# Gated mix of dilated attention and a spectral filter: a new issue order for the second half of the kernel

## The chip, the cores and the metric

The kernel runs on one core of a Trainium2 chip. The metric is device time in microseconds (us). The kernel before took 452.81 us as a median of 3 runs (452.49 to 456.78).

## The reference

The input x has S = 2048 rows of D = 640. Branch a is attention with 32 heads of 20: each row attends to 8 rows at distances 0, 2, ..., 14 behind it. Branch b is a 2-D Fourier transform, a multiplication by a complex weight, and the transform back. A gate mixes them.

```python
qkv = (x @ wqkv).reshape(B, S, 3, H, Dh)             # H = 32, Dh = 20
idx = pos[:, None] - (jnp.arange(8) * 2)[None, :]    # mask = idx >= 0
logits = einsum("bhsd,bhswd->bhsw", q, k[idx]) * Dh ** -0.5
o = einsum("bhsw,bhswd->bhsd", softmax(where(mask, logits, -1e9)), v[idx])
a = o.reshape(B, S, D) @ wo
b = irfft2(rfft2(x) * (w_r + 1j * w_i), s=(S, D))
g = sigmoid((x * gate_w).sum(-1, keepdims=True))
return g * a + (1 - g) * b
```

## The kernel before

All 16 row blocks j lie as row = 16 p + j on the 128 partitions p, so that a block is every 16th row. The work has these stages, most of which overlap.

1. **qkv.** TensorE (PE) multiplies x by wqkv, in a first half for even j and a second for odd j, each in four groups of heads. ScalarE (ACT) copies each bank to a tile `ev` and stores it to a DRAM tensor `qkvd`. Until about 239 us PE does little else.
2. **attention** (`attend`), for eight heads groups per half, named by unit and letter (7a, 7b, 6a, 6b, 5a, 5b, 4a, 4b are those of the second half, in the order in which they run). For each, `kt`, `vt` (600 KB each) and `q` are loaded from `qkvd` into a ring of six buffers; the products `pr` and their sums `L` are made mostly on VectorE (DVE); a softmax follows; the products `pv` are made on GpSimd (POOL) and summed to `o` on DVE, which is stored to a DRAM tensor `od`.
3. **frequency stage** (`freq(g)`, 16 steps, in the order 1, 2, 3, 0, 4, ..., 15; from 238 to 350 us). A step makes, in PE, `v` and `u` (bank 0 and bank 1), in ACT a copy `vs` of v, in DVE `ab` = u + vs and u − vs, which frees u's bank, in PE `x` and `z` from ab and a table `mm`; ACT copies x to the first third of a tile `P`, and multiplies x and z by a sign into `X`, whose two halves two DMAs on ACT's queue (160 KB each, 64 partitions) exchange into the rest of P. Then POOL multiplies P by the weight `wp` of this step (642 KB, loaded by SyncE, SP, into one of two buffers) and adds two thirds of it, DVE multiplies z by wp, subtracts P's last third (z−P in the text), and forms two sums `s`; a small ACT step completes s; PE makes `g` from s, and ACT copies g to `zg`. Step 0 makes `ix` and `iz` in place of the exchange.
4. **project_even**, mixed into it: `ot` is loaded, transposed on PE (`oTp`), split into two parts `oT` by ACT and DVE, multiplied by wo (`woa`, `wob`), scaled by the gate on ACT, and stored to `ad`.
5. **spatial** (350 to 407 us) makes the rows of b from zg (`oa`, `ob`, `ha`, `hb`); the even blocks are finished there with what `ad` holds.
6. **project_odd** (407 to 447 us) does the output projection of the odd blocks and the last stores.

The order of all this isn't the order in which the code calls the engines. Each call of an engine is recorded as one of 3614 operations (`Plan.record`); `Plan.order` then takes them from that list by a table of positions, `ORDER`, a compressed text of bytes; and `Plan.issue` runs them in this order, with the framework's own scheduling switched off. The framework puts in the semaphore waits that the data and the buffers ask for. Each engine has one queue that it works off in order, and a DMA waits in the queue of the engine that issues it: `kt`, `wp`, `mm`, `ot` and the stores of `o` on SP's, `vt`, `q`, P's exchange and the stores of `ev` on ACT's (`ON_ACT`). Which buffer or bank a tile gets is settled when it is recorded, so ORDER doesn't change that: x is always bank 2, z banks 3 and 4 in turn, g bank 5, the projection bank 6.

In the profile all recorded calls show one line, L400, except those of `Engine.run`, which are L177. So the profile is read by the names of tiles.

Of the kernel before, what the change touches and what calls it, by code (L numbers as in the profile page):

```python
# [17 lines left out]
S, D = 2048, 640  # L18
# [213 lines left out]
%*_v{Ta_^3=d<&1(R>`cY~)FfJAaBz1ZK0I<N^-e7(pzkO~FPz<-dP(x(IlwVBqSbRRT5rYgu1T6G{2<I~O<a=YYl0Jk$QP{l|_cUTx1sL~IU#-qKQc=BZ{n4m`EvZF&VD8v<QobTp<#G}S-$H`Uf3  # L232
lV6!!5tQ?X+VqEQ;48Q$_J_73PWOHP+BCYo8Y-^CjsRGKe*zWp49~VEfz?XhfDFHGoCqv^_Kpn;y4>(MBVz{ny;&9IO*)|MYVG9JncXGFPoic<`y=IEWte%CmWSp+Y(?B){u46!4sOair&o<;_Iq~K
3>`-kmHW$~uf>&2Jr05V5nspNt;nTvSO|#fz%QF~8X35h0g$l!JgO6RW!C68drMU&X5A6P=$Nr$+3jJPJ}uOj?=*n19-86hl;LN8Hhf<GxhI&winTZQ>2x;|-suR*5NzR*Uwo9z+eSs6vga>nZOwBG
vLfUmcstXVX;$<mV<B7Oc8{(9Pt{1C13guny)&_~q%$t2kz5)^-d8^>eAsZ7EM8Oz;y?j{zH-yTJHejC*-FFaYuSxIKkree?rYC2bW3W_yQgR@e#A)4&MXBfmOcKy<E&!!vdXd)`5M^&Pegrjt213<
Q1^7bAKaX_6D=5&6d7EIuzq~__@DxEGE=WG9(#$x0LH^-vD``kI}fUGW#|^h!u*`Ow@P$|J8B%p1zm`(grJuCIIT_GfcsAk1)l!3HXU)~?U7qYNO_Gt=w3t$jG%dd9Ksr=<wp6LB)ZQ%4A4SWObh;*
RA!!7t1p4B+tN0OgLygfxAScXYQ}vlM0eBD7jso~Egme7wu9n*bYoWZaMo7mVp<GIX3?0zZYCA!ock-4_(6CTPAT38Wm{e?u^lZ`vF^p9erqZ-v89)N$1@>Xn{+x$m;6b?f;>#{pWCaqKGa+g1*;||
y<<yQ!&N=^1CqrpZk90@j&LGJlMyy|(BBp8S4Z|duoIc_X4s{yRYN!c6BFn)jKjNf+n>dr`qn_B!u=Q;@co)GBq81xMJ~cha0hAP0y)*5W4}Cj@=It+Cf${fI(`t`M89Nxs$Vl%p}!usDSWi-uamq9
L1H6jJsz(u8~3MqodIHL;4J<ohmAh|OK6kI=+dnk16>ll98S}@JD_@ZhOMd^K9&;5ptMQZBLWPdk`^UuL+0omK_Fii#f4`Xo+AK;_(LC7aA~!Fl<nAx#H(0DQzYEM>)N5b`vSea*aqcSl%7Uj`|-fA
FUi#-xiXER^66kMImz$qNq=rK!`8u~G0J@ZJ@P-@fTNQsIW?MNXZwXEsg6Q(=D|UndsuDw=~=(?v4L<eD8lBDP<p7no7pdR>YOVFQMJn{rAGTH^V&3iq8BYdi_<gCcvH5KRaOs15p^lK%&*eDlACo=  # L240
C}*H&-g&0j)St4GreIZ#TG<*aimDSC%*Wm!vxsIxMEGFWrL0@IrF;1NGOduo<C2jV{m$zFYTsK?^-^@_gB`nBms`c+Qah%wZdv=fl@uAEJw%WhqN^<m*#OCC_}dQq_(TG(ABO)+HgKRq$=Gh)F1+Y`
lHF?dsJb7>dEXJ&4d~Gs#`=ro&!=@;z<{yT^bd}5Be+?zs#~Ztr(l5sjrQR7p?SdQQWAX~@^a@zEiy=Jv6Qpe?xiC<;1YQ8Dmtm%aps*@&NhcJr6S;SMZB$?V4JHAtJ|wpQN97*0>>cg@94#?97E>z
pU?&YRWjdFygm~3=6}?Kf~mXd(yFa%=t&aIYHN?fCEkN+dp1y%Le$TZH5w~(eNLzW@Ff=olKJzr&i$JZF3vp|$YJx@d<+Am+-cw+ve-2t*@=hYn6MRi@LbzaaNrVM1`Z;P41*KiKeL?G@uR^-1MZ5x
&-8t7Du9l>se=sPCxLnNh;^qjLG5`BXp?n1mOQv_foF~PmrIp0URDZ9y{AxbCEqx~gc22Kl55n9iKb3pmM2AFl?9s<%V_(F=6&<AHu-VupN1gQiTtv^$=dzAPsK$unsZLvi(M{|@Mz<GZ0vG`-R8y^
bv7z~Pg0O1gkLeUqgQeq5%2C9*y`mtKUd+!)|0D2@BdqV%JHrxltS?Np2LNOjj#QLWP*&p4jikEFT4al``Go?Z{aiaW^}2=gL^VNQjc}d4svyvlHJEWdz*EN&g_ArzPjuAQS1(S$C_w%7ZL_JLexHo
6Nw65Rol(|>9&}$FY9Hfijtts{9>(rn|i6b10=LY`g-?C(t1(9$sqZ0Pd+5CM$WOG0Jg>}Y_c&Glxk0Odj1Gzb;g+@my_})V2Rc%Nz|V44};O+VX~t%-R<B?XKlQm38e~G=F)4bm$ln-fu}=g!uu-G
IKE@Ycb{9`szhQr(gLm`%k>!i3IdZbL>|0ftSvP1#mIxlvXh}b9V*=7i#LRT_9KBgCyF3iP9s+^s8;{19)Lqti(_Z}%cQw&3E<#UCl%!M_^OH1bF#vSJJH1%@-m~}l-EXb`>QMDbJR1<??VJ#_D+S|
??F>fX_^NI<G5n+MgCe4u+1FXcTLFiPK-*-@1Sq@L=T{l182WS+Oxj#uuSg{fI(h!=ZeSZwm<`)>5FR?WShdG9839FRJIn1L_=AM@N(se=&hn2tB88b;iE<#$}VZFq((Q)8~YVvIs~+jLJd3k1I^ig
e!Vj#k`-!U!L?8Ec{a#98LT5<5pd1T<I-RrilniF3~47HcQ1`iO1<O;g1m*{1_;S#Jy-{rb|4l(8c7UFl^~}jU}pt--wC&3>=)and8<&7T#&>10000000I6Oyf^>={WXEXr~nH50ssI2003E9
"""  # L250


# [725 lines left out]
```

## Time and profile before

| | us |
|---|---|
| median of 3 runs | 452.81 (452.49 to 456.78) |
| profiled execution | 453.08 |
| its span (first to last instruction) | 451.0 |
| PE busy | 435.0 (96%), 2576 instructions |
| DVE busy | 409.1 (91%), 519 |
| POOL busy | 363.2 (81%), 318 |
| ACT busy | 214.9 (48%), 593 |
| mean granted clock of PE | 1.000 |

The time is 2.08 us longer than the span; the profile doesn't show that part. Busy time is an average over stages with different limits, and matmuls are pipelined with modelled ends, so the idle time in front of single PE instructions, and what ended it, says more than the 96%. A wait for several semaphores is put down to the one that came last by the profile, which can be the wrong one where the named engine had long been done.

### The profile page before, as it was taken

The numbers are of one execution on the slowest core, as the hardware profiler recorded it, in microseconds if no ns is written. First come the engines' busy times: TensorE is split into PE (matmuls) and PEld (weight loads), VectorE is DVE, ScalarE is ACT, GpSimd is POOL, SyncE is SP. The second block draws the span as 40 slices with busy tenths as digits, with TensorE's granted clock in tenths as the row PEclk, the third lists the DMA queues.
The fourth block names the chain that finished last, engine by engine and source line by source line (L and its number), as shares of the span: only waits on it lengthen the run. The fifth ranks groups of instructions, "written<-read, shape, count | busy, mean of one in ns | idle before, by whom it ended". The sixth has DMA issues, their size and how long they took to land. (4 is left out here: it accounts for less than half of the span.)

```text
span 451.0 us, 7548 instructions
## 1 busy us (share of the span) xinstructions
PE 435.0 (96%) x2576; PEld 384.9 (85%) x2576; DVE 409.1 (91%) x519; ACT 214.9 (48%) x593; POOL 363.2 (81%) x318
## 2 busy tenths in 40 slices
PE   9999999999999999999998989799998999999996
PEld 6888878888888888899886869698977899989996
DVE  4999999999999999999999776898988999887775
ACT  5543144462325355245547657486754665552110
POOL 1247987999999897989998695689988998889920
PEclk9999999999999999999999999999999999999999
DMA  8999797989487999978969969899864732276653
GB/s 324 389 340 331 236 383 221 326 242 367 128 220 233 297 286 302 308 202 260 294 194 293 329 204 278 235 305 263 254 198 130 248 108 69 81 227 197 187 200 118
DMA packets 73958, 110.60 MB, mean 245 GB/s; under 512 B 21297, under 2 KB 50993, under 8 KB 73921
## 3 DMA queue, kind: packets, MB, share of 16 engines
q1 hardware_dynamic: 40192, 69.16, 47.7%
q10 hardware_dynamic: 32816, 36.97, 27.4%
q0 software_dynamic: 912, 4.00, 2.4%
q8 instruction: 20, 0.33, 0.3%
q14 instruction: 18, 0.14, 0.1%
HBM read 72.34 MB, written 32.84 MB: 233 GB/s over the span
## 5 line engine op out<-in xcount | busy, mean ns | idle before, releaser
L400 PE MATMUL qkv<-w,xo 128*128 128x480 f32 (+1 forms) x480 | 116.5, 388 | 0.3 <-ACT zg L400 0.2
L400 PE MATMUL qkv<-w,xe 128*128 128x480 f32 (+1 forms) x474 | 106.6, 382 | 1.1 <-ACT ev L400 1.1
L400 PEld LDWEIGHTS qkv<-w,xe 128*128 128x128 f32 x474 | 89.2, 189 | 16.8 <-ACT ev L400 2.0
L400 PEld LDWEIGHTS qkv<-w,xo 128*128 128x128 f32 x480 | 88.5, 189 | 13.6 <-ACT zg L400 0.7
L400 ACT COPY ev<-qkv 128x480 f32<-128x480 f32 x64 | 34.8, 560 | 56.4 <-PE qkv L400 47.2
L400 PE MATMUL wob<-wo,oT 128*128 128x320 f32 x240 | 50.8, 327 | 0.0
L400 PE MATMUL woa<-wo,oT 128*128 128x320 f32 x240 | 50.4, 327 | 0.0
L400 POOL TENSOR_TENSOR P<-P,wp 128x963 f32<-128x963 f32 (+1 forms) x16 | 35.2, 2199 | 16.9 <-DMA P<-X 11.3
L400 PEld LDWEIGHTS woa<-wo,oT 128*128 128x128 f32 x240 | 37.7, 189 | 0.9 <-DVE oT L400 0.5
L400 PEld LDWEIGHTS wob<-wo,oT 128*128 128x128 f32 x240 | 37.8, 188 | 0.6 <-issue 0.2
L400 POOL TENSOR_TENSOR fx<-fx 128x158 f32<-128x158 f32 (+1 forms) x16 | 12.3, 784 | 25.4 <-DVE fx L400 18.5
L177 PE MATMUL ob<-gt,zg 64*128 64x161 f32 (+2 forms) x160 | 27.7, 327 | 0.0
L177 PE MATMUL oa<-gt,zg 64*128 64x161 f32 (+1 forms) x160 | 27.6, 327 | 0.0
L400 ACT CAST oT<-oTp 128x384 fp32r<-128x384 f32 (+1 forms) x32 | 13.1, 426 | 28.7 <-PE oTp L400 17.0
L177 PEld LDWEIGHTS oa<-gt,zg 64*128 64x128 f32 x160 | 23.7, 186 | 3.1 <-issue 0.7
L400 PE MATMUL g<-mm,s 128*128 128x128 f32 x150 | 24.8, 278 | 1.3 <-ACT s L400 0.7
L400 POOL TENSOR_TENSOR w<-raw,w 128x480 fp32r<-128x480 f32 (+1 forms) x20 | 25.9, 1306 | 0.0
L400 PEld LDWEIGHTS g<-mm,s 128*128 128x128 f32 x150 | 21.8, 190 | 3.6 <-ACT zg L400 1.0
L400 DVE TENSOR_TENSOR oT<-oTp,oT 128x384 fp32r<-128x384 f32 (+1 forms) x32 | 15.4, 488 | 9.6 <-ACT oT L400 9.3
L400 PE MATMUL u<-bt,zc 128*128 128x240 f32 (+2 forms) x96 | 21.0, 324 | 3.0 <-DVE ab L400 3.0
L177 PEld LDWEIGHTS ob<-gt,zg 64*128 64x128 f32 x160 | 23.8, 186 | 0.0
L400 ACT CAST w<-raw 128x480 fp32r<-128x480 f32 (+1 forms) x30 | 17.4, 594 | 12.6 <-DMA raw<-in_wqkv 6.4
(307 smaller groups left out, 1131.2 us busy)
## 6 DMA issues: line engine op xcount, KB each, us to landing
qkvd<-ev ACTq DMA_DIRECT2D x32, 480.0 KB, 4.9
wp<-in_ws SPq DMA_DIRECT2D x16, 642.0 KB, 5.6
raw<-in_wqkv SPq DMA_DIRECT2D x25, 240.0 KB, 5.4
fx<-in_x SPq DMA_DIRECT2D x8, 641.0 KB, 7.1
ot<-od SPq DMA_DIRECT2D x16, 320.0 KB, 4.1
P<-X ACTq DMA_DIRECT2D x30, 160.5 KB, 4.2
fd<-fx POOLq DMA_DIRECT2D x6, 640.0 KB, 5.3
f<-fd SPq DMA_DIRECT2D x6, 640.0 KB, 6.4
```

Of the source, the lines that this page charges most:

```text
L177: getattr(self.real, name)(*a, **k)
L400: p.dve.memset(w, 0.0)
```

## The change

Only the text of `ORDER` differs. The first 1765 of the 3614 operations stay; of the 1849 behind them 1729 stand at another position, half of them by 5 places or less, nine in ten by 32 or less, the farthest by 343. Every engine has the same instructions as before. Each engine's first difference lies between 223.9 us (PE) and 230.2 us (DVE) in the time of the kernel before.

```diff
 ORDER = """
-{Wp48S^xk5{}S0j0stWa8~^|S5YJf5;2b*)YFz*T0sAKZbW)=m>G~>ja#c?We=xxA
...
+{Wp48S^xk5{}S0j0stWa8~^|S5YJf5;2b*)UtItI0sAKZbW)=m>G~>ja#c?We=xxA
...
```

Three places show what moved. The number in a name is that of the step, or the unit and letter of the heads (`pr5a4`: heads 5a, rows 4); the last number counts tiles and stays the same.

The first is on DVE, in steps 5 and 8 of the frequency stage. Before:

```order
L400 TENSOR_REDUCE o7b4_497<-pv7b6_499 128x160
L400 TENSOR_TENSOR z5_676<-z5_676,wp5_665 128x321
L400 TENSOR_TENSOR z5_676<-z5_676,P5_674 128x321
L400 TENSOR_TENSOR pr5a4_538<-kt5a_532,qbank_63 128x1280
L400 TENSOR_TENSOR ab8_710<-u8_709,vs8_708 128x321 x2
L400 TENSOR_TENSOR s5_686<-P5_674,z5_676 128x5x64 x2
```

After, on the same engine:

```order
L400 TENSOR_REDUCE o7b4_497<-pv7b6_499 128x160
L400 TENSOR_TENSOR ab8_710<-u8_709,vs8_708 128x321
L400 TENSOR_TENSOR z5_676<-z5_676,wp5_665 128x321
L400 TENSOR_TENSOR pr5a4_538<-kt5a_532,qbank_63 128x1280
L400 TENSOR_TENSOR ab8_710<-u8_709,vs8_708 128x321
L400 TENSOR_TENSOR z5_676<-z5_676,P5_674 128x321
L400 TENSOR_TENSOR s5_686<-P5_674,z5_676 128x5x64 x2
```

Both halves of ab of step 8, and pr5a4, now stand ahead of the instruction that reads P of step 5. On POOL, two multiplies pv6a0 have moved to the place ahead of P of step 5 (and what they need, L6a times s6a, ahead of P of step 3). On SP the load of kt5b has moved from behind the load of wp6 to behind that of wp2, 11 places earlier.

The second place is ACT's queue between qkv and the frequency stage, where vt6a is loaded. Before:

```order
L400 ACTIVATE X2_621<-z2_620,sign_325 128x321
L400 COPY zc0_637<-zg_211 128x48x4
L400 COPY vs3_625<-v3_624 128x321
L400 ACTIVATE zc0_637<-zg_211 128x48x4
L400 DMA P2_618<-X2_621 64x642 x2
L400 COPY P2_618<-x2_619 128x321
L400 DMA vt6a_501<-qkvd_64 128x1200
L400 DMA qkvd_64<-ev4_6_323 128x6x160
```

After:

```order
L400 COPY ev4_4_320<-qkv4_5_321 128x6x80
L400 DMA qkvd_64<-ev4_4_320 128x6x160
L400 DMA q5a_534<-qkvd_64 128x640
L400 COPY qbank_63<-q6b_518 128x160
L400 DMA vt6a_501<-qkvd_64 128x1200
L400 COPY zc1_602<-zg_211 128x384
```

The load of vt6a has moved from behind P of step 2 to the copies of the last qkv banks, ahead of P of step 1. The load of vt6b, which stood between P of step 1 and P of step 2, now stands behind P of step 3, ahead of vs5.

The third place is ACT's queue near the end of the frequency stage. Before:

```order
L400 ACTIVATE s12_780<-z12_769,P12_767 128x1
L400 COPY vs15_801<-v15_800 128x321
L400 ACTIVATE ya8_848<-woa8_849,g_73 128x320
L400 ACTIVATE X14_797<-z14_796,sign_325 128x321
L400 DMA P14_794<-X14_797 64x642 x2
L400 COPY P14_794<-x14_795 128x321
```

After:

```order
L400 ACTIVATE s12_780<-z12_769,P12_767 128x1
L400 DMA vt5b_549<-qkvd_64 128x1200
L400 ACTIVATE ya8_848<-woa8_849,g_73 128x320
L400 ACTIVATE X14_797<-z14_796,sign_325 128x321
L400 COPY P14_794<-x14_795 128x321
L400 COPY vs15_801<-v15_800 128x321
L400 DMA P14_794<-X14_797 64x642
L400 COPY qbank_63<-q4a_566 128x160
L400 DMA P14_794<-X14_797 64x642
```

The load of vt5b stood behind the last g of the stage; now it stands ahead of P of step 14, whose two DMAs have two ACT copies more ahead of them, and one between them. Elsewhere in PE's order, x of step 4 stands ahead of z of step 4, and a v matmul of step 3 ahead of x of step 2; on DVE, t of step 0 stands behind z−P of step 3.

More of the change, by code (lines that the diff above doesn't have):

```diff
@@ L222 @@
 ORDER = """
-{Wp48S^xk5{}S0j0stWa8~^|S5YJf5;2b*)YFz*T0sAKZbW)=m>G~>ja#c?We=xxAfB@%${{m#x=b59`IdyTU{vq(yT@9sNe+BS{#HY+m)y=f!_RR8qRRBGA*}EW<uG2O+6A~}&R!D}&rV+x2jv1iJ
+{Wp48S^xk5{}S0j0stWa8~^|S5YJf5;2b*)UtItI0sAKZbW)=m>G~>ja#c?We=xxAfB@%${{m#x=b59`IdyTU{vq(yT@9sNe+BS{#HY+m)y=f!_RR8qRRBGA*}EW<uG2O+6A~}&R!D}&rV+x2jv1iJ
 <-;gAir31;1Wf;>N>_o7_jkA<(T8Z}8f9+iVn*m~XGw&Dh4Q!g^!a-g;gRa_JDi6k#N9Iq<cZ2&JtcN76xX8*H9m++$L@A2#7kr>_z#tF%`KR?`)4zIcgHuNs+E`A0h0RujinI`1a|acnWK|Ere?@m
@@ L234 @@
 3>`-kmHW$~uf>&2Jr05V5nspNt;nTvSO|#fz%QF~8X35h0g$l!JgO6RW!C68drMU&X5A6P=$Nr$+3jJPJ}uOj?=*n19-86hl;LN8Hhf<GxhI&winTZQ>2x;|-suR*5NzR*Uwo9z+eSs6vga>nZOwBG
-vLfUmcstXVX;$<mV<B7Oc8{(9Pt{1C13guny)&_~q%$t2kz5)^-d8^>eAsZ7EM8Oz;y?j{zH-yTJHejC*-FFaYuSxIKkree?rYC2bW3W_yQgR@e#A)4&MXBfmOcKy<E&!!vdXd)`5M^&Pegrjt213<
-Q1^7bAKaX_6D=5&6d7EIuzq~__@DxEGE=WG9(#$x0LH^-vD``kI}fUGW#|^h!u*`Ow@P$|J8B%p1zm`(grJuCIIT_GfcsAk1)l!3HXU)~?U7qYNO_Gt=w3t$jG%dd9Ksr=<wp6LB)ZQ%4A4SWObh;*
-RA!!7t1p4B+tN0OgLygfxAScXYQ}vlM0eBD7jso~Egme7wu9n*bYoWZaMo7mVp<GIX3?0zZYCA!ock-4_(6CTPAT38Wm{e?u^lZ`vF^p9erqZ-v89)N$1@>Xn{+x$m;6b?f;>#{pWCaqKGa+g1*;||
@@ L238 @@
[L238 to L249, printed above, removed]
+vLfUmcstXVX+;I|zA<K_j}gV#Y!WNY{{+th<9!`zZp9Qbuyo3|?%M^X%JMtja)#YJ?0Wu?C3|7heNpzzNVsdyf^jS^d5EL;7!gZ{mpMNB4Eog0mKm1?%&?YhifjiJ+WsK*uke%>;o$nSuZ~QtdR8qZ
@@ new lines @@
+sFn@jY!=scvP^xj45X(oupXhV$gAes*6pTQn(V?ZWTVQSv(G5kFQap|AAIxumA2W@CJkzeNN5n|+8(ysoh631UroY@8($&y9R=O|iVF=#r{j#dC@1n#yU%L3g-{aE^{PYf@<?MUvV3J1ch>NDVK|M&
+dn(8qarH>hSZAgOeZR7rwZKP{_47puSwoU2geH)WmFDLyM*)ux%>W?fNuw9Y>_*Yp@s=}+%((t1G)Bt<m<p=;x*oLUVGTOZUGY|2P&CY*e2p2IEU>Nk93;q46;oyV`=mD{`!jzZ2((~d-Ay}Xn(4qP
+{u|v7Ep-V&<lh#+O*E110f1EX5P;DW4}7za_e9YE-UBV-iKQcp{fAo|)Qt>FdPeJ*t1NYaY(%EjPpqezPYJy~iNowP$Spp|;Mkj<MR;)rj0yG)e1?lWKiJ26)_0%_gLukJ3Z+Ei3;RQ)Ow?kdvG-`{
+kvSMk%|*!N!wKJJuO_!BS~L8>=T-gF;bt51C(lFb876-+s?V39+YMk&TA=`2iW76p;mnd+|0Is2;ClLRpuVY<;Gg;~Nt%bMT$^3M@FHkD*ctz%HOA(<6!CeW6w24_(c`G96ev!D7YTX>#}qBhN+(gO
@@ new lines @@
+D6I)E-Q(zEOFg(EGC_%!KI-tz3tyEU=PUFjbdr5N@MSdVlXp>RE`N6aLU@gPS!zhH2X92XagxqA)En;ljspP<*Xp>((O3TMy|p>erYZFk{@{!xn@<F@8r~{Usxd@3za<dn%fmMsFK#mI0HNI^7&oj?
+Bb+5*(po9`WEB(P(5v}|W#=Z5HW7&Pd0hmr`+dk*!ksPK4SfZ*-11}V(6{&7x=ZSSVA|2SQzQHhmq!oHBzs<EiFlO)wsQ>9xhH>Pry?pXU^SLLmcb17wX?DrW#RPtg1<Ri#7N}1+3CAX!t&!<WPuX-
+L~=fl?`q@pefc@o@5%_bSQQ*iB>@!rYq|yKRwJO1hi`pgm=vjYSC?v{lF|PodnoL^)sW59LjO0_6gAtf(mLwlRb6S~&+utyN?;?BiTafqd<p=N3E~r2wCLTkaU}-+gq(pwKc10`tJ#Fa-i_J2GWIXz
+q9G7!4|`s26XmGRiPB;S={E<f(GZsdM%2b|h@Ah9(2r}nWrB1D0G_w5#$-#p>Hm~|t>IByRG;1i>8gb>TYOa|6j)vzmThH4F>9&=Y)qs{v(R(-G@i0aKFSxw?O_eIg;Uu?HK0o}EuR7w$oAC=lAF|l
@@ new lines @@
+Uq2G{S}o`&C9Cy>I4=2Z_}%*z0j%7k;Vs}ezH`g%I!)7ml<OVF_+Pc3eFt<vbstX%(HpljI9pJ<;8y=KYXU7Jed9(`F@X%5!9X=}d{M$%);50y6*3M4mGQ+i*OCSk@Lho51J}SPvWK#wo0eyIg4Mh5
+ArMG`{LCPTz&dX4(zOnev>+fF)l9Wy`91XZNpG=g(9+fz3`P>)DxvOsBA(uHr%9ZIC8%5P=Wwftm3TX|(7Qr6jLid)eM=*1)ERJ4$+Pp~LQN!QEkABxNfN&WYLR&ibUGd<j79GfhRU6Im4JDHyr~9q
+R%t#2X<kA;fAc>^XKpP+!N0(VjKeV4Dn!ftztv}fmURWB?tCBpdJmTv^QUb5b+fP*>v$C&!>A{5T{8hV`vLAtiA>e~)0Ohg%~G$-1ci68aQ^+Gb!;yj${a^3`->_^94w>UFYWxj^9Y);lsMc(OZ)j`
+EtKRbu9!RqtPb7P*CY)M&q*;}j6cq(+(?gfe#P2K>^f*orVGgYF2iEIex++}>Th4+!khxWfqF&pq+X1V4ShUzUNUwRhW)9aCS*dslj+0WZR1D`E*ZxVO(gZhZ_%VMMx1>$v$lllaeN35t@bybU;Vh;
@@ L250 @@
+BmMg>ElH2Oi2x#A*KI)A@J<68kK@T_>^|NcqT=m~pPkdk%eE#5y0ZR%A_jdRD|&kTraT~NbIv5b84cJ>uC+jZz#`<uq4}Z1-`Qsu<Y{1<;B@h-e>rHSh6<@`NGOXJAWD4f*5bT^P#HU4l)21RJiDG&
+dW9zDN~Nq_l}cm+TAY$l`+Sc^?t_@)olOLQOy3HA0&G9E1B;JspnIO}Ie8_cl?P^;q>T`08!Wx8-Gg`h{D0V5W~T71WgRn22><{900HwDyf^>=BPJhxr~nH50ssI2003E9
 """
```

## The prediction

> **What bounds the kernel now.** I read the busy times first, then the stretches, then the waits of the busiest engine, and last what stands behind each wait.
>
> ```profile
> PE 435.0 (96%) x2576; PEld 384.9 (85%) x2576; DVE 409.1 (91%) x519; ACT 214.9 (48%) x593; POOL 363.2 (81%) x318
> ```
>
> TensorE (PE) does matmuls in 435.0 of 451.0 us. The order of its instructions is the same up to 223.9 us, so all that the change can do is done behind that. (Where a time is given for an instruction at its new place, it is the time at which its new neighbours ran before.) These are eight stretches from 225 us to the end; the columns are start:end, length, busy time of PE, of its weight loads, of VectorE (DVE), ScalarE (ACT) and GpSimd (POOL), the granted clock, the busy share of the DMA engines and GB/s.
>
> ```profile
> 225.00:245.00 20.00, 19.27 (x95) 16.19 (x93) 20.00 (x20) 11.93 (x40) 18.78 (x17) 1.00 0.77 252
> 245.00:262.00 17.00, 14.95 (x81) 12.37 (x80) 12.15 (x22) 9.54 (x28) 12.68 (x9) 1.00 0.94 276
> 262.00:287.00 25.00, 21.33 (x135) 18.92 (x136) 20.29 (x35) 16.51 (x52) 17.25 (x17) 1.00 0.84 251
> 287.00:328.00 41.00, 41.00 (x269) 37.23 (x267) 37.14 (x61) 29.05 (x84) 35.36 (x27) 1.00 0.89 268
> 328.00:351.00 23.00, 20.18 (x129) 17.44 (x130) 20.35 (x32) 11.27 (x31) 20.32 (x15) 1.00 0.54 151
> 351.00:405.00 54.00, 53.85 (x505) 49.86 (x501) 50.26 (x71) 31.47 (x94) 49.56 (x40) 1.00 0.50 151
> 405.00:447.00 42.00, 41.48 (x292) 40.81 (x291) 32.76 (x70) 7.57 (x19) 24.86 (x27) 1.00 0.57 180
> 447.00:451.00 4.00, 0.39 (x3) 0.13 (x1) 0.55 (x1) 0.00 (x0) 0.00 (x0) 0.96 0.31 112
> ```
>
> Length less busy time gives PE's idle time: 0.73, 2.05, 3.67, 0.00, 2.82, 0.15, 0.52 and 3.61 us, together 13.55. The last 3.61 are the store after the last matmul, which stays. So about 9.9 us can be gained at the very most, and nearly all of it lies in three stretches of the frequency stage, 245 to 287 and 328 to 351. The clock is full there, so it takes no part. Those idle times, by instruction (start, duration, what ran, in brackets the idle time before it and who ended it):
>
> ```profile
> 241.71 0.78 PE L400 MATMUL x<-ab,mm 128*128 128x321 f32 x2 [0.73 <-DVE ab L400]
> 246.00 0.81 PE L400 MATMUL x<-ab,mm 128*128 128x321 f32 x2 [0.93 <-ACT P L400]
> 259.70 0.78 PE L400 MATMUL z<-ab,mm 128*128 128x321 f32 x2 [0.49 <-DMA mm<-in_t_mm]
> 262.97 1.35 PE L400 MATMUL iz<-ab,tbfirst 128*128 128x321 f32 x4 [1.50 <-ACT s L400]
> 285.07 0.64 PE L400 MATMUL u<-bt,zc 128*128 128x240 f32 x2 [2.62 <-DVE ab L400]
> 331.90 0.67 PE L400 MATMUL u<-bt,zc 128*128 128x240 f32 x2 [0.37 <-DVE ab L400]
> 333.07 0.81 PE L400 MATMUL z<-ab,mm 128*128 128x321 f32 x2 [0.51 <-ACT s L400]
> 345.07 0.93 PE L400 MATMUL g<-mm,s 128*128 128x128 f32 x6 [0.74 <-ACT s L400]
> ```
>
> The largest is u of step 9 at 285.07. It needs the bank that u of step 8 held, and that one is free when DVE has made ab of step 8. What DVE did then:
>
> ```profile
> 278.79 0.49 DVE L400 TENSOR_TENSOR z<-z,wp 128x321 f32<-128x321 f32 x1
> 282.23 0.50 DVE L400 TENSOR_TENSOR z<-z,P 128x321 f32<-128x321 f32 x1 [2.95 <-POOL P L400]
> 282.64 1.48 DVE L400 TENSOR_TENSOR pr5a<-kt5a,qbank 128x1280 f32<-128x1280 f32 x1
> 284.03 0.89 DVE L400 TENSOR_TENSOR ab<-u,vs 128x321 f32<-128x321 f32 x2
> ```
>
> DVE stood 2.95 us at z−P of step 5, and ab of step 8 was queued behind it though its inputs were there. What it waited for:
>
> ```profile
> 279.96 2.23 POOL L400 TENSOR_TENSOR P<-P,wp 128x963 f32<-128x963 f32 x1 [5.27 <-ACT zg L400]
> ```
>
> The releaser named, an ACT copy, had nothing to do with P; POOL stood 5.27 us for P of step 5, whose two exchanged halves were still in flight:
>
> ```profile
> wp<-in_ws SPq DMA_DIRECT2D x1, 642.0 KB, 5.0
> kt5b<-qkvd SPq DMA_DIRECT2D x1, 600.0 KB, 7.7
> P<-X ACTq DMA_DIRECT2D x2, 160.5 KB, 6.6
> ```
>
> These are the transfers issued between 271 and 273 us: 6.6 us for 160 KB beside 1.2 MB of other loads.
>
> **The change, part by part.** No instruction comes or goes, so the sum is made of waits alone.
>
> *A, u of step 9.* DVE now makes ab of step 8 before it waits for P of step 5, with pr5a between its two halves. From 278.79 the queue is 0.45 (half of ab's 0.89), 0.49, 1.48, 0.45, which ends at 281.7. PE came to u of step 9 at 285.07 − 2.62 = 282.45, so ab comes some 0.7 us before PE asks for it; I take −2.5, which leaves 0.1 at the bank. The cover is that nothing ahead of ab waits; if DVE is itself late by 3 us there, the gain is nothing, and more than the 2.62 can't be had. z−P of step 5 then runs at 281.7 or when P is ready, no later than its 282.23 of now, because kt5b no longer loads beside P, and POOL fills its 5.27 us with two multiplies pv6a that were behind.
>
> *B, iz and z around 260.* PE waits 1.50 for s of step 3 and 0.49 for a table. P of step 3 was late too, and POOL stood for it:
>
> ```profile
> 258.59 2.22 POOL L400 TENSOR_TENSOR P<-P,wp 128x963 f32<-128x963 f32 x1 [4.03 <-DMA P<-X]
> mm<-in_t_mm SPq DMA_DIRECT2D x1, 480.0 KB, 7.0
> P<-X ACTq DMA_DIRECT2D x2, 160.5 KB, 5.4
> vt6a<-qkvd ACTq DMA_DIRECT2D x1, 600.0 KB, 4.3
> ```
>
> (The two rows in the middle are issues of 251 to 254.5 us, the last one of 245 to 247.) In 245 to 262 the DMA engines are 0.94 busy at 276 GB/s: the stretch is full, and what is taken out of it moves up what is behind. vt6a now goes out near 228 us (with the copies of the last qkv banks), which takes 600 KB (614 kB) away: 614 kB / 276 GB/s = 2.2 us. The small stores that went with it stay near their places, and vt6b comes in at about 256, behind P of step 3. I take −1.5: all of iz's wait would fit in the 2.2 us, the table's 0.49 I leave, since z of step 4 now also stands behind x of step 4 and z−P of step 3. Bounds: 0, if P of step 3 is then held by POOL, which has one more multiply (L6a) ahead of it, and −2.0.
>
> *C, the two x at 241.71 and 246.00.* A v matmul moves into the first gap, worth 0.4; the second is held by ACT's copy of P, which is not moved up. Taken as 0.
>
> *D, the earlier loads.* kt5b and vt6a now share 229 to 241 with the weights of the first steps and P of step 1. ACT also issues that P's halves behind three casts and copies more. If one of the two loads falls ahead of P of step 1, it is late by the 2.2 us of 600 KB; PE needs it only through s of step 1, and DVE, which makes that, is 20.00 of 20.00 us busy there, so that its own queue decides. The engines' share of 0.77 leaves 0.23 × 20 = 4.6 us of room for the 4.4 us of both. Bounds 0 and +2.2; I take 0, by that room.
>
> *E, vt5b.* Its 600 KB were issued at 350 us, when the frequency stage was over:
>
> ```profile
> vt5b<-qkvd ACTq DMA_DIRECT2D x1, 600.0 KB, 4.3
> P<-X ACTq DMA_DIRECT2D x2, 160.5 KB, 5.5
> ```
>
> Now it goes out on ACT's queue at about 333 us, right ahead of P of step 14, whose two halves took the 5.5 us of the second row. This P is on the chain that ended last, without slack, and leads through POOL, DVE and ACT to g of step 14, for which PE waits 0.74 already:
>
> ```profile
> 334.98 5.51 DMA P<-X
> ...
> 340.65 2.27 POOL P L400
> ```
>
> What is late here is late at the end. Two prices add up. First, the halves are now issued behind the copy of x into P and behind vs of step 15, two ACT copies, later by
>
> ```profile
> 332.92 0.42 ACT L400 COPY vs<-v 128x321 f32<-128x321 f32 x1
> ```
>
> 0.84 us in all. Second, the traffic: rows with a 600 KB load near them take 7.7 (kt5b above) where this one took 5.5, at most 2.2 more. Near P of step 6, though, which was behind vt5a in the same queue, it was
>
> ```profile
> vt5a<-qkvd ACTq DMA_DIRECT2D x1, 600.0 KB, 7.4
> P<-X ACTq DMA_DIRECT2D x2, 160.5 KB, 6.7
> ```
>
> only 1.2 more, at a share of 0.84, and the share here is 0.54. I take half of the 2.2, so E is 0.84 + 1.1 = +1.9, with bounds of 0 (the ACT copies hidden by an earlier z of step 14, the traffic free) and +3.0. [...]
>
> *F, the rest.* The waits 0.37 and 0.51 near 332 hang on P of step 12, the same chain one round earlier; its multiply by wp is only moved within DVE's waiting time. Behind 351 us, PE is idle 0.67 us in 96, and the new order changes little there. 0.
>
> Sum: −2.5 − 1.5 + 1.9 = −2.1. The profiled execution took 453.08 us; less 2.1 it is 451.0. It stands 0.27 above the median of 452.81, so the forecast is 450.7.
>
> **The rivals.**
>
> *More is kept* (to about 448): vt5b hides in the idle DMA share, E is 0, C gives its 0.4 and B its 2.0. 452.81 − 2.5 − 2.0 − 0.4 = 447.9. For it speaks the 0.54 share in 328 to 351, against it that E's chain has no slack.
>
> *Nothing is left* (452.8): PE runs ahead by 2.5 us at u of step 9 and gives it back at the next thing that is not moved up with it, the chain of P of step 12, which goes through DMA, POOL, DVE and ACT in turn; POOL is 35.36 of 41.00 us busy in 287 to 328 and DVE 37.14. Against it: PE has no idle time at all there, so it is the slowest of them.
>
> *Slower* (457.2): the loads ahead of P are the mechanism, at two places. vt5b delays P of step 14 by the full 3.0, and kt5b with vt6a delay P of step 1 by 2.2, which reaches PE; P of step 3 is no earlier then (B is 0), and A keeps a third, 0.8, because DVE runs late too. 452.8 + 3.0 + 2.2 − 0.8 = 457.2. It decides from 2.5 + 1.5 = 4.0 us of delay at the two places together, where A and B are used up. For it: P's 5.4 to 6.7 us where the DMA engines are 0.84 to 0.94 busy. Against it is this row, from 241.9 to 245.9 us, where vt6b and vt6a went out on P's own queue, one ahead and one behind it:
>
> ```profile
> vt6b<-qkvd ACTq DMA_DIRECT2D x1, 600.0 KB, 4.0
> ...
> P<-X ACTq DMA_DIRECT2D x2, 160.5 KB, 2.6
> ```
>
> **How the numbers follow.** Forecast 0.44 (449.3 to 452.2); more kept 0.24; nothing left 0.20; slower 0.12. A measurement of this kernel can tell about 1%, 4.5 us: faster is below 448.3, slower above 457.3. The case "more kept" is at 447.9 and lies on the edge; with half of it and a little of the forecast's lower end, and since all the waits together would be worth 9.9, faster is 0.25. Slower by over 1% needs all that the slow rival has and a little more, 0.08. The rest, 0.67, is within. The range holds the forecast, "nothing left" and most of both others: 447.0 to 455.5.
>
> **What would show it.** In the changed kernel's profile: the wait of u for ab falls from 2.62 to under 0.3 (A); iz waits under 0.3 and P of step 3 lands some 2 us earlier (B); the transfer of P of step 14 takes 6.5 to 7.7 us and g of step 14 waits 2 to 3 us instead of 0.74 (E); the stretch 287 to 328 stays without idle time. If that last stretch shows new waits for POOL or DVE, the gain of A went there and "nothing left" holds. Wrong would be a forecast whose idle sum falls by 4 us or more, or one in which P of step 1 makes PE wait before 250 us.

## The result

The changed kernel takes 450.52 us as a median of 22 runs (448.2 to 456.03), the kernel before in the same sessions 455.06 us (451.85 to 458.75). The ratio of the two is 0.9905, with a 95% interval of 0.9884 to 0.9927: 0.95% less time, some 4.3 us, twice the 2.1 us that the prediction summed. (Slow runs, over 1.5% above the fastest of the same kernel, such as the one at 456.03, are left out of the ratios and of all counts and averages further below.) The predicted 450.7 us is nearly the measured median, but partly by chance: the 452.81 us that it started from, a median of 3 runs, lies 2.2 us under the median that the kernel before shows over more runs.

The profiled execution of the changed kernel took 453.87 us, with a span of 452.1 us and a mean granted clock of 0.996. That is 3.4 us above its own median, while the profiled execution of before (453.08 us) was 2 us below its own. So these two profiles, laid side by side, show no gain at all, and what the change does must be read wait by wait. The busy times of the changed kernel, from its page, and the stretches of it that answer to those shown of before (the last three columns are the granted clock, the share of the DMA engines and GB/s):

```profile
PE 436.8 (97%) x2576; PEld 386.0 (85%) x2576; DVE 408.1 (90%) x519; ACT 215.3 (48%) x593; POOL 363.8 (80%) x318
```

```profile
225.00:245.00 20.00, 19.93 (x98) 16.87 (x97) 19.97 (x21) 11.35 (x35) 18.10 (x17) 1.00 0.90 302
245.00:262.00 17.00, 14.90 (x82) 12.00 (x80) 12.20 (x21) 10.80 (x35) 13.31 (x9) 1.00 0.91 250
262.00:287.00 25.00, 23.27 (x134) 20.22 (x135) 20.72 (x35) 15.86 (x47) 21.10 (x20) 0.93 0.76 226
287.00:328.00 41.00, 39.74 (x256) 36.13 (x255) 35.19 (x58) 27.68 (x80) 31.09 (x24) 1.00 0.87 262
328.00:351.00 23.00, 21.20 (x139) 18.43 (x137) 21.52 (x33) 12.26 (x35) 21.12 (x17) 1.00 0.75 221
```

PE's idle time in them is 0.07, 2.10, 1.73, 1.26 and 1.80 us, 6.96 in all, where it was 9.27. In the third stretch the clock is 0.93, where it was 1.00. The main waits of PE in the changed kernel, in order of time (three more, of 0.46 to 0.58 us, stand at 304.22, 340.16 and 341.50):

```profile
246.51 0.78 PE L400 MATMUL x<-ab,mm 128*128 128x321 f32 x2 [1.10 <-DVE ab L400]
249.48 0.94 PE L400 MATMUL v<-bt,zc 128*128 128x240 f32 x4 [0.56 <-ACT vs L400]
263.26 0.81 PE L400 MATMUL z<-ab,mm 128*128 128x321 f32 x2 [1.34 <-DVE t L400]
264.43 2.22 PE L400 MATMUL iz<-ab,tbfirst 128*128 128x321 f32 x4 [0.36 <-ACT s L400]
285.04 0.57 PE L400 MATMUL u<-bt,zc 128*128 128x240 f32 x2
320.59 0.81 PE L400 MATMUL z<-ab,mm 128*128 128x321 f32 x2 [0.80 <-ACT s L400]
345.68 0.94 PE L400 MATMUL g<-mm,s 128*128 128x128 f32 x6 [0.59 <-ACT s L400]
```

The u of step 9 (at 285.04) has no wait left; it had 2.62. The iz waits 0.36 instead of 1.50, but z of step 4 just ahead of it now waits 1.34, where its table cost 0.49. It waits for DVE's t of step 0, which in the new order stands behind z−P of step 3, and that one waited 3.59 us for POOL's P in this execution. And g of step 14 waits 0.59, not more than the 0.74 of before. DVE around ab of step 8, in the changed kernel:

```profile
281.93 0.48 DVE L400 TENSOR_TENSOR ab<-u,vs 128x321 f32<-128x321 f32 x1
282.33 0.49 DVE L400 TENSOR_TENSOR z<-z,wp 128x321 f32<-128x321 f32 x1
282.73 1.48 DVE L400 TENSOR_TENSOR pr5a<-kt5a,qbank 128x1280 f32<-128x1280 f32 x1
284.12 0.48 DVE L400 TENSOR_TENSOR ab<-u,vs 128x321 f32<-128x321 f32 x1
284.52 0.49 DVE L400 TENSOR_TENSOR z<-z,P 128x321 f32<-128x321 f32 x1
```

These are the five instructions in their new order, without a stop, and z−P of step 5 no longer waits for POOL (it waited 2.95). POOL's multiply of P of step 5 has no wait either, where it had 5.27; the two pv6a stand ahead of it:

```profile
278.89 2.70 POOL L400 TENSOR_TENSOR pv6a<-vt6a,L6a 128x640 f32<-128x640 f32 x2
281.45 2.27 POOL L400 TENSOR_TENSOR P<-P,wp 128x963 f32<-128x963 f32 x1
```

### The profile page after: what moved, and what is told of

The parts are those of the page before. It is cut to its first block, busy times and chain, and to the rows that moved or that the text cites. A ratio compares the mean times of both kernels' runs of the same rounds, so it can differ in the third digit from the quotient of the medians.

```text
span 452.1 us, 7560 instructions
## 1 busy us (share of the span) xinstructions
PE 436.8 (97%) x2576; PEld 386.0 (85%) x2576; DVE 408.1 (90%) x519; ACT 215.3 (48%) x593; POOL 363.8 (80%) x318
## 5 line engine op out<-in xcount | busy, mean ns | idle before, releaser
L400 PE MATMUL wob<-wo,oT 128*128 128x320 f32 x240 | 49.7, 325 | 0.0
L400 PE MATMUL v<-bt,zc 128*128 128x240 f32 (+2 forms) x96 | 21.5, 326 | 1.0 <-ACT vs L400 0.6
```

The costliest lines, as they stand in the source:

```text
L400: p.dve.memset(w, 0.0)
```

## The experiments

Three questions: which part of the order gains, whether the early load of vt5b costs what I said, and where the other 2 us come from. All kernels below compute the same thing; only the order differs, but for one that also moves a load to another queue. A cut means: the one order up to a position in the list of operations, and behind it what is left, in the other order.

### Three parts of the order

The first three kernels put one part of the new order into the order before: up to 267 us, from there to some 290 us, and from there to 351 us.

```diff
 e1_early:   order = new[:2100] + what is left, as before
 e2_middle:  order = before[:2100] + new[:2330] + what is left, as before   (kt5b kept behind wp6)
 e3_late:    order = before[:2330] + new[:2815] + what is left, as before
```

> The new order up to the last matmul of step 0's iz (some 267 us), then the order before. It has the early loads of kt5b and vt6a and vt6b's later one, and not the new place of ab of step 8, nor the early vt5b. My sum: iz's wait of 1.50 goes, the u of step 9 still waits about 2.6: -1.5 us against the kernel before. Rival (the loads are what counts): -3 to -4, nearly all that the whole change gave (0.9905 of the time before, some -4.3 us), because landings no longer decide in steps 0 to 5. Rival (the early loads only delay P of step 1): 0 to +2.

> The order before up to 267 us, then the new order up to some 290 us, then the order before; kt5b stays right behind the load of wp6. So ab of step 8 stands ahead of the wait for P of step 5, and two pv6a ahead of P of step 5 on POOL, while all big loads are where they were. My sum: the 2.6 us wait of u of step 9 goes to 0.1, and the time falls by 2.5 us. Rival (a gain there is given back at the next wait): the wait goes, and new waits of 2 us or more appear between 287 and 351 us; time 0 to -0.5. Rival (the loads count): -1 or less, since P of step 5 lands as late as before.

> The order before up to some 290 us, then the new order up to the end of the frequency stage (351 us), then the order before. It has vt5b ahead of P of step 14 and the other moves of that stretch. My sum: P of step 14 takes 6.5 to 7.7 us instead of 5.5, g of step 14 waits 2 to 3 us instead of 0.7, time +1.9 us. Rival (the load is hidden in the idle share of the DMA engines): P of step 14 takes at most 6, g waits under 1, time 0 to -0.5. Rival (the stretch is itself better): -1 to -2.

Measured against the kernel before: early 0.9936 (0.9906 to 0.9965), middle 0.9930 (0.9900 to 0.9959), late 1.0014 (0.9990 to 1.0039). The middle part gives some 3 us, a little more than the wait of u of step 9. The early part gives as much, but not at the place where I had looked for it. Its profile's waits of PE at iz and at u of step 9:

```profile
263.37 1.35 PE L400 MATMUL iz<-ab,tbfirst 128*128 128x321 f32 x4 [0.37 <-ACT s L400]
...
284.09 0.64 PE L400 MATMUL u<-bt,zc 128*128 128x240 f32 x2 [1.23 <-DVE ab L400]
```

The wait of iz has fallen to 0.37, and the u of step 9 waits 1.23 instead of 2.62 although DVE's order there is the old one: without kt5b beside it, P of step 5 lands 5.9 us after its issue instead of 6.6, and POOL waits 3.93 for it instead of 5.27. Counted from a matmul that all kernels share, at about 222 us, iz ends after 41.98 us in the kernel before and after 42.16 us here, so up to iz nothing is gained; at u of step 9 it is 62.73 and 61.54. In the late part, P of step 14 did land later; its transfers, POOL's wait and PE's wait for g of step 14 are

```profile
P<-X ACTq DMA_DIRECT2D x2, 160.5 KB, 6.3
```

```profile
340.64 2.26 POOL L400 TENSOR_TENSOR P<-P,wp 128x963 f32<-128x963 f32 x1 [2.24 <-DMA P<-X]
345.06 0.94 PE L400 MATMUL g<-mm,s 128*128 128x128 f32 x6 [1.32 <-ACT s L400]
```

6.3 us instead of 5.5, and 1.32 instead of 0.74: 0.6 us where my sum had 1.9, and in the time 1.0014, which can't be told from nothing.

### The load of vt5b, put back

```diff
 L400 ACTIVATE s12_780<-z12_769,P12_767 128x1
-L400 DMA vt5b_549<-qkvd_64 128x1200
 L400 ACTIVATE ya8_848<-woa8_849,g_73 128x320
...
 L400 COPY zg_211<-g15_3_815 128x32x8
+L400 DMA vt5b_549<-qkvd_64 128x1200
```

> The new order, with the load of vt5b alone put back behind the last g of the frequency stage. My sum: 1.9 us faster than the changed kernel, and g of step 14 waits under 1 us; against the kernel before some -6. Rival (hidden): the same time as the changed kernel within 0.5 us, -4 to -4.5 against the kernel before, P of step 14 lands no earlier.

0.9914 (0.9880 to 0.9948): the same as the changed kernel. P of step 14 takes 4.1 us without vt5b ahead of it and 4.9 us with it (the first row is of this kernel, the second of the changed one), and g of step 14 waits 0.46 and 0.59.

```profile
P<-X ACTq DMA_DIRECT2D x2, 160.5 KB, 4.1
```

```profile
P<-X ACTq DMA_DIRECT2D x2, 160.5 KB, 4.9
```

### Single moves

```diff
 f1_kt5b_early (SP):
 L400 DMA wp2_611<-in_ws 128x1284
+L400 DMA kt5b_548<-qkvd_64 128x1200
 L400 DMA wp3_622<-in_ws 128x1284
...
 L400 DMA wp6_678<-in_ws 128x1284
-L400 DMA kt5b_548<-qkvd_64 128x1200
```

> The order before, with the load of kt5b alone moved up on SyncE's queue, right behind the load of wp2. If this load is what keeps P of step 5 in flight: P of step 5 takes some 5.5 instead of 6.6 us, u of step 9 waits 1 to 1.5 instead of 2.6 us, -1 to -1.5 us. If all of the early part's gain (0.9936) is this load: -2.5 to -3. If it only moves the jam to steps 1 and 2: x or z of those steps wait 1 us more, time 0.

1.0028 (0.9998 to 1.0059), no gain. At u of step 9 the wait falls from 2.62 to 1.67, nearly as expected, but time is lost earlier: P of step 1 takes 4.6 us (2.5 before), P of step 3 takes 6.2 us (5.4 before), the table of step 4 lands after 8.9 us (7.0 before), and z waits 2.39 us for it (0.49 before).

```profile
262.94 0.78 PE L400 MATMUL z<-ab,mm 128*128 128x321 f32 x2 [2.39 <-DMA mm<-in_t_mm]
...
286.57 0.65 PE L400 MATMUL u<-bt,zc 128*128 128x240 f32 x2 [1.67 <-DVE ab L400]
```

```profile
mm<-in_t_mm SPq DMA_DIRECT2D x1, 480.0 KB, 8.9
P<-X ACTq DMA_DIRECT2D x2, 160.5 KB, 6.2
```

```diff
 f2_ab_ahead (DVE):
+L400 TENSOR_TENSOR ab8_710<-u8_709,vs8_708 128x321
 L400 TENSOR_TENSOR z5_676<-z5_676,wp5_665 128x321
+L400 TENSOR_TENSOR pr5a4_538<-kt5a_532,qbank_63 128x1280
+L400 TENSOR_TENSOR ab8_710<-u8_709,vs8_708 128x321
 L400 TENSOR_TENSOR z5_676<-z5_676,P5_674 128x321
-L400 TENSOR_TENSOR pr5a4_538<-kt5a_532,qbank_63 128x1280
-L400 TENSOR_TENSOR ab8_710<-u8_709,vs8_708 128x321 x2
```

> The order before with five VectorE instructions alone in a new order: ab of step 8, z times wp of step 5, pr5a4, ab of step 8, z minus P of step 5. All loads and POOL's order stay. If the place behind the wait is the cause of the stall by itself: u of step 9 waits under 0.3 us although P of step 5 lands as late as before, and the time falls by 2.5 to 3 us. If the late P comes back at the next consumer: u's wait goes, g of step 5 or the z behind it waits 1.5 us or more, time -0.5 to -1.

0.9942 (0.9920 to 0.9965), some 2.6 us from five instructions. The u of step 9 starts 60.14 us after the shared matmul instead of 62.73, without a wait. But the late P comes back at the z that follows, which needs s of step 5:

```profile
285.25 0.81 PE L400 MATMUL z<-ab,mm 128*128 128x321 f32 x2 [1.25 <-ACT s L400]
```

So both answers of the expectation are partly right: the stall went, half of it returned one step later, and the time still fell by all of it. What makes up for that half is shown below, under the clock.

```diff
 f3_vt6a_early (ACT):
 L400 DMA qkvd_64<-ev4_4_320 128x6x160
+L400 DMA vt6a_501<-qkvd_64 128x1200
...
 L400 COPY P2_618<-x2_619 128x321
-L400 DMA vt6a_501<-qkvd_64 128x1200
```

> The order before, with the load of vt6a alone moved up on ACT's queue to right behind the store of the bank pair ev4_4 (some 227 us). If it is this load that keeps P of step 3 late: iz waits under 0.5 instead of 1.5 us, P of step 3 takes under 4.5 instead of 5.4 us, -1 to -1.5 us. If the order of PE, DVE and POOL there is the cause: iz still waits over 1 us, time 0.

0.9949 (0.9920 to 0.9978), some 2.3 us. P of step 3 takes 2.9 us where it took 5.4, and between 247 and 283 us its timeline shows no wait of PE; iz ends after 39.61 us instead of 41.98. The stall of u of step 9 is as it was:

```profile
P<-X ACTq DMA_DIRECT2D x2, 160.5 KB, 2.9
```

```profile
283.37 0.97 PE L400 MATMUL u<-bt,zc 128*128 128x240 f32 x2 [2.76 <-DVE ab L400]
```

### Sums of parts

```diff
 f4_early_middle:  order = new[:2330] + what is left, as before
 g1_ab_and_vt6a:   the edits of f2_ab_ahead and f3_vt6a_early together
 g2_kt5b_back:     the new order, kt5b put back behind the load of wp6
```

> The new order up to some 290 us, the order before behind that: the early and the middle part without the late one. If the two parts gain at different waits they add: -6 us against the kernel before (0.9936 and 0.993). If they overlap at u of step 9 (the early part alone left 1.2 us of its wait): -4.5 to -5 us. If the late part takes back something (1.0014 alone): 0.5 us less time than the changed kernel, else the same.

> The order before with two moves alone: the five VectorE instructions around ab of step 8 (0.9942 by themselves) and the load of vt6a to some 227 us (0.9949 by itself). Six instructions moved in place of 1729. If these two are the whole of what the change gives: 0.989, the same as the changed kernel or a little less, with neither the wait of u of step 9 nor that of iz. If the other moves carry something too: 0.9925 or more. If the two overlap: the same, 0.994.

> The changed kernel with the load of kt5b alone put back behind the load of wp6. Moved alone it gave 1.0028. If its early place costs something in the changed kernel too (the table of step 4 landing late): 0.5 to 1 us less time than the changed kernel, 0.988 to 0.989. If it gains there because P of step 5 lands earlier: 0.993. If VectorE's new order has made P of step 5 indifferent: 0.9905.

Early and middle together give 0.9905 (0.9876 to 0.9935), just what the whole change gives: the late part and what follows it give nothing that these runs can tell, and the two parts don't add to the 6 us that they give one by one. What they have in common is shown below, under the clock. Six moved instructions (g1) give 0.9914 (0.9879 to 0.9948), the same within the interval as the 1729 that the change moved. None of these beats the changed kernel beyond its interval. In g1 the z behind u waits 1.86 us, since P of step 5 still flies beside kt5b (6.9 and 8.0 us from issue to landing):

```profile
283.07 0.81 PE L400 MATMUL z<-ab,mm 128*128 128x321 f32 x2 [1.86 <-ACT s L400]
```

With kt5b back in its old place, the changed kernel takes 0.9959 (0.9929 to 0.9989) of the time before. So its early place, which gave nothing by itself, seems to be worth some 2 us in the new order; the interval only just leaves that of the changed kernel. In its profile g of step 14 waits 1.27 us where the changed kernel has 0.59, and the waits of z of step 4 and of iz (1.32 and 0.37) are like those of the changed kernel; this doesn't make 2 us, and stays open.

### How a load in the same queue delays P

```diff
 g3_vt5b_at_P14 (ACT):
 L400 ACTIVATE s12_780<-z12_769,P12_767 128x1
-L400 DMA vt5b_549<-qkvd_64 128x1200
...
 L400 COPY vs15_801<-v15_800 128x321
+L400 DMA vt5b_549<-qkvd_64 128x1200
 L400 DMA P14_794<-X14_797 64x642

 g4_vt5b_on_SP: the load of vt5b on SyncE's queue, in the order behind wp15
-        self.queue("vt").dma_start(vt.rearrange(...), rows(2, 0, 15))
+        (S if nm == "5b" else self.queue("vt")).dma_start(vt.rearrange(...), rows(2, 0, 15))
```

> The changed kernel with the load of vt5b moved down on ACT's queue to right ahead of the first half of P of step 14, so that it has no lead (it was issued 1.7 us ahead of it). If a ring is worked off in order: both halves land 1.5 to 2 us later than in the changed kernel, whose halves took at most 5.6 us, so some 7 us; g of step 14 waits 2 us or more, +1.5 us. If the load costs only a share or nothing: the halves take at most 6 us, time within 0.5 us of the changed kernel.

> The changed kernel with the load of vt5b put on SyncE's queue behind the load of wp15, which is issued within 1 us of P of step 14's halves. If only the order within one ring counts: the halves take no more than in the changed kernel (5.6 us), time the same within 0.5 us, and vt5b itself takes longer, 6 us or more. If all traffic counts alike: the halves take 6.5 to 7 us, as with the load right ahead of them on ACT's queue.

Right ahead of P in one queue, vt5b costs all that I had feared, and more: 1.0005 (0.9979 to 1.0031), which takes back the whole gain. (It was issued 0.55 us ahead of the first half.) On the other queue it was issued 0.54 us behind the first half of P, and P's halves are as fast as without it. The transfers (first of g3, then of g4), and what follows in g3 on POOL and PE:

```profile
vt5b<-qkvd ACTq DMA_DIRECT2D x1, 600.0 KB, 3.9
P<-X ACTq DMA_DIRECT2D x2, 160.5 KB, 7.3
```

```profile
vt5b<-qkvd SPq DMA_DIRECT2D x1, 600.0 KB, 7.1
P<-X ACTq DMA_DIRECT2D x2, 160.5 KB, 4.2
```

```profile
340.39 2.23 POOL L400 TENSOR_TENSOR P<-P,wp 128x963 f32<-128x963 f32 x1 [3.66 <-DMA P<-X]
344.77 0.94 PE L400 MATMUL g<-mm,s 128*128 128x128 f32 x6 [2.94 <-ACT s L400]
```

So P's halves take 4.1 us without vt5b, 4.2 with it on the other queue, 4.9 with it 1.7 us ahead on their own, and 7.3 with it right ahead on their own. Each of these is one execution, and others spread: in the kernel before they took 5.5 without the load, and in e3, with the load 1.7 us ahead, 6.3. Only the 7.3 stands clear of all of them. The 7.3 agrees with the first answer that was expected of g3, that a queue (a ring, as it says there) is worked off in order: vt5b landed 3.9 us after its issue, the halves issued behind it after 7.3. How two queues share the DMA engines isn't shown. vt5b took 7.1 us instead of 3.9 on SyncE's queue, but it stood there 0.38 us behind the load of wp15, which itself took 5.5; P beside it was hardly slower, 4.2 for 4.1. The time of g4, 0.9959 (0.9931 to 0.9987), is above that of the changed kernel all the same. Its profile can't show why, since the profiled execution (449.49 us, a span of 447.7, g of step 14 waiting 0.77) is 2.5 us under g4's own median, and this stays open too.

### The clock behind a wait

The profiles of g3, f3 and g1 show something that the profile of before had hidden. These are stretches of 1 us behind the wait of u of step 9 in f3; the third column from the right is the granted clock:

```profile
283.00:284.00 1.00, 0.63 (x2) 0.60 (x3) 1.00 (x4) 0.00 (x0) 0.06 (x1) 0.78 0.87 282
284.00:285.00 1.00, 1.00 (x5) 0.94 (x5) 1.00 (x3) 0.89 (x4) 1.00 (x1) 0.50 1.01 379
285.00:286.00 1.00, 1.00 (x4) 0.66 (x3) 0.87 (x1) 0.24 (x1) 1.00 (x1) 0.50 1.00 408
286.00:287.00 1.00, 1.00 (x5) 0.83 (x4) 0.00 (x0) 0.53 (x1) 0.18 (x1) 0.52 0.23 93
287.00:288.00 1.00, 1.00 (x8) 0.79 (x7) 0.00 (x0) 0.63 (x2) 0.00 (x0) 1.00 0.00 0
```

PE waits 2.76 us, starts again, and then has half its clock: what is missing from 1.00 in the rows adds up to 1.7 us, so the half clock lasts 3.4 us. The same u in the profile of before kept 1.00 behind its 2.62:

```profile
285.00:286.00 1.00, 0.93 (x6) 0.90 (x6) 1.00 (x3) 0.19 (x2) 0.42 (x1) 1.00 0.88 313
286.00:287.00 1.00, 1.00 (x7) 0.67 (x6) 1.00 (x2) 0.97 (x5) 1.00 (x1) 1.00 1.02 408
```

In the profile of g3, where the long wait is that of g of step 14, the low clock is there:

```profile
346.00:347.00 1.00, 1.00 (x7) 0.90 (x6) 0.87 (x3) 0.23 (x1) 1.00 (x2) 0.63 0.00 0
347.00:348.00 1.00, 1.00 (x6) 1.00 (x5) 1.00 (x4) 0.46 (x3) 1.00 (x2) 0.50 0.00 0
348.00:349.00 1.00, 1.00 (x6) 1.00 (x5) 1.00 (x1) 0.15 (x2) 1.00 (x2) 0.50 0.02 8
```

And in the profiled execution of the changed kernel it stands behind the 1.34 of z of step 4, which accounts for 1.7 of the 3.4 us by which that run was over the median (the profile of g2 has the same, behind 1.32):

```profile
265.00:266.00 1.00, 1.00 (x4) 0.61 (x3) 0.53 (x1) 1.00 (x4) 1.00 (x2) 0.50 0.29 118
266.00:267.00 1.00, 1.00 (x5) 0.80 (x4) 0.31 (x1) 0.64 (x2) 1.00 (x3) 0.50 0.00 0
267.00:268.00 1.00, 1.00 (x7) 1.00 (x6) 0.98 (x3) 0.00 (x0) 1.00 (x1) 0.50 0.00 0
```

Every run reports its mean granted clock, and one such loss takes 1.7 of 450 us, 0.0038, from it. So I counted the runs at 0.996 or less (the longest wait of PE behind 223 us is from the one profile of each kernel):

| kernel | longest wait of PE | runs | at 0.996 or less |
|---|---|---|---|
| before | 2.62, u of step 9 | 85 | 59 |
| e3_late | 3.05, u of step 9 | 11 | 9 |
| f3_vt6a_early | 2.76, u of step 9 | 12 | 10 |
| f1_kt5b_early | 2.39, z of step 4 | 12 | 7 |
| g3_vt5b_at_P14 | 2.94, g of step 14 | 10 | 8 |
| g1_ab_and_vt6a | 1.86, z after u of step 9 | 8 | 2 |
| f2_ab_ahead | 1.73, iz | 12 | 0 |
| e2_middle | 1.64, z of step 4 | 9 | 0 |
| changed kernel | 1.34, z of step 4 | 21 | 3 |
| g2_kt5b_back | 1.32, z of step 4 | 12 | 3 |
| e1_early | 1.23, u of step 9 | 12 | 1 |
| e4_vt5b_back | 1.10, x of step 2 | 8 | 1 |
| g4_vt5b_on_SP | 1.10, x of step 2 | 10 | 3 |
| f4_early_middle | 1.10, x of step 2 | 6 | 0 |

Kernels with a wait of 2.39 us or more are at 0.996 or less in most of their runs, 93 of 130, those with at most 1.86 us in 3 of 10 or fewer. (The waits are those of one execution each, and where in a run the clock was lost is known only for the profiled ones.) The five moved instructions of f2, which take the long wait away and leave all loads alone, bring 59 of 85 to 0 of 12; g3, which makes a long wait at another place, brings it back there, to 8 of 10. The runs of before at 0.996 or less take 454.94 us on average, the others 452.76: 2.18 us apart.

With that the two open sums close. These are the averages of the runs at over 0.996 alone, and how far they lie under the 452.76 of before: f2 451.76 (1.0), the early part 451.25 (1.5), the middle part 450.98 (1.8), early and middle together 449.89 (2.9), the changed kernel 450.17 (2.6). So of the 2.6 us of f2 only some 1.0 is the stall, whose other half returned, and the rest is the low clock that it no longer has. And at full clock the early and the middle part nearly add, 1.5 and 1.8 to 2.9; what both save, and can be saved but once, is the low clock.

## Why the prediction was right or wrong

**The range and the sign** held: 450.52 lies in 447.0 to 455.5, and within 1% was the likeliest class. Of the signs that were named, A's came (no wait at u of step 9), B's not (iz waits 0.36, but P of step 3 took 6.8 us instead of 5.4), and E's not (4.9 us and 0.59). The sum was half of what was measured, −2.1 for −4.3 us, and several of its terms were off in ways that cancelled.

**A, u of step 9, −2.5**, was right in cause: moved alone, the five instructions make u start 2.6 us earlier and give 0.9942. Its size is another matter: at full clock the move alone is worth some 1.0 us, and the rest of the 0.9942 is clock. I had named late P as harmless to z−P; it was not as long as kt5b loads beside it (1.25 us at the next z in f2, 1.86 in g1). In the changed kernel, where kt5b is gone from there, no wait followed at that place.

**"The clock is full there, so it takes no part"** is the step that failed most: the sum had no term for the clock. It is true of the one execution that I read, and not of 59 of 85. Besides its own 2.62 us in the profile, the long wait at u went with some 2.2 more in 59 of 85 runs. Of runs at over 0.996 alone, the kernel before has an average of 452.76 us and the changed one 450.17, which is −2.6, near my sum. The rest is that the low clock became rare: 59/85 × 2.18 = 1.5 us before, and 3 of 21 runs at 2.5 us more, 0.4 us, after. Together that is −3.7 of the −4.3; the runs are from several sessions, so the split is good to about half a us.

**B, iz and the table, −1.5.** The mechanism was right, and its size was too small: vt6a alone, moved early, makes iz end 2.4 us earlier. But in the changed kernel iz ends no earlier than before.

**C and D, 0**, hold what takes it back. D's mechanism came: P of step 1 takes 4.6 us instead of 2.5 with kt5b moved alone (f1), and 4.1 to 5.0 in five profiles with the changed kernel's order up to there (e1, e4, f4, g3, g4); with vt6a moved alone (f3) it takes 2.5. As expected, little of that reaches PE: a z at some 251 us waits up to 0.60 in the five and 0.83 in f1. C's first gap closed (0.73 before, at most 0.29 in the five), but x of step 2 waits 1.10 (0.93 before), and a v at some 249 us and a g at some 256 us, which had no wait, 0.56 and up to 0.37. So iz ends after 41.4 to 42.4 us in the five, where it was 41.98, although z of step 4 and iz together wait only 0.60 to 0.86, where it was 2.0. In the changed kernel's own profile and in that of g2 it is the other way round: P of step 1 takes 2.6 us, but P of step 3 6.8 and 6.7 (4.2 to 4.5 in the five), z of step 4 waits 1.34 and 1.32, and iz ends only after 43.49 and 43.33 us. Since g2 has kt5b back in its old place, kt5b isn't what makes P of step 3 late there; what does stays open. Nor are the 2.39 us that z waits for its table in f1 all due to kt5b: in the four executions with the order of before up to there (before, f2, e2, e3) it waits 0.26 to 1.64. What the early place of kt5b bought is the earlier P of step 5. The 0.9936 of the early part comes from that (1.23 us at u of step 9) and from the rarer low clock, not from iz.

**E, vt5b ahead of P of step 14, +1.9**, was the term with the wrong size. Its price of the traffic set unlike things side by side: the 7.7 us is the time of kt5b itself, and the halves of P of step 5 beside it took 6.6, which is 1.1 over the 5.5. That half of the wrong 2.2 is 1.1 too was luck. The order within the queue was seen (7.3 us with the load right ahead in g3, 4.2 with it on the other queue in g4), but the load was issued 1.7 us ahead, which was nearly enough: 0.1 to 0.6 us at g of step 14, and nothing that e4 can tell in the time. Nor do the two ACT copies show: e4 keeps them ahead of P's halves, and g of step 14 waits 0.46 there. I had the order of the queue, and hadn't worked out the lead in time.

**F, 0**: the late part as a whole gave 1.0014, which agrees.

**The rivals.** "More is kept" was nearest in size: 4.9 us where 4.3 were measured, and E was indeed hidden; but it had no clock in it. "Nothing left" came true in f2 and g1 by half at one place only; in the changed kernel the stretch 287 to 328, which was to stay without idle time, has 1.26 us of it, 0.80 at a z that waits for s, but in g4 it has 0.05. The mechanism of "slower" exists, as g3 shows, and the change kept clear of it by 1.7 us of lead.

## What to carry to other kernels

A long wait of PE cost more than its length here, because the clock could be low behind it: 0.50 for 3.4 us behind the 2.76 us of f3, though 1.00 behind the 2.62 in the profile of before (its runs at 0.996 or less took 2.18 us more). A single profile can miss that, so look at the granted clock of all runs before calling the clock full. Look for the instruction that waits on a late transfer, and at what stands behind it on its engine with its inputs ready: DVE stood 2.95 us at z−P here with ab behind it, and moving five instructions (f2) gave 0.9942. A load right ahead of an urgent transfer in the same queue made it 3.2 us later here (7.3 for 4.1), most of the load's own 3.9; with a lead of 1.7 us it was 0.8 (4.9). On the other queue the transfer was no later (4.2), though the kernel as a whole was not faster for it (0.9959).

## What the runs showed of the hardware

That PE's clock would be halved behind a wait was not expected. Kernels with waits of 2.39 to 3.05 us were at 0.996 or less in 93 of 130 runs, and in the profiles of g1, the changed kernel and g2 waits of 1.86, 1.34 and 1.32 us were followed by the low clock.

The traces of the changed kernel and of before show a grid in time. In that of the changed kernel the clock of 0.50 behind z of step 4 lasts 3.41 us, and it begins 76.0 times that length after the first entry of the trace's record of the clock. Behind the last matmul each record has one more stretch of 0.50: in before from 450.64 us of the span, 130.0 times that length after the first entry, in the changed kernel from 452.49, just behind the span's end, 131.0 times. The first entry lies at 5.35 us of the span in the one and at 6.91 in the other, so in these two the grid does not begin with the program, and the same wait can fall differently on it from run to run. For f3, g1 and g3 the points of the grid are reckoned here from where their low clock begins, in steps of 3.41 us: 283.56, 283.90 and 346.26 by their rows of 1 us. In f3, g1 and the changed kernel the waits of 2.76, 1.86 and 1.34 lie wholly between two points of it, and the next stretch has the half clock. In the profile of before, which kept the full clock there, a point of it cuts the wait of u of step 9 in two (0.95 and 1.68 us). But g3's wait, which lost clock, is cut too (1.01 and 1.92). So where the wait falls seems to matter; how much idle time between two points is enough no run here shows.
